# Batch 0's queries in three blocks of 256, one of them mixed of even and odd chunks, in a kernel of clustered attention and a gated feed-forward network

## The chip, the cores and the metric

The kernel runs on one core of a Trainium2 chip. The metric is the device time of one execution in microseconds (us). A core has five engines with a queue each: TensorE (PE, matrix products; the loading of a product's stationary operand is shown apart as PEld), VectorE (DVE), ScalarE (ACT, exponentials and other functions), GpSimd (POOL) and SyncE (SP). Any of SP, ACT and POOL can issue transfers (DMAs), which then run beside the engines. Matrix products write to PSUM, which here has eight banks of 128 rows by 512 numbers of 32 bits.

## What is computed

Four batches (B) of 768 tokens (S) with 8 heads (H) of 64 numbers (D). Each query and key belongs to the nearest of 16 centroids of its head (by the cosine), and a query sees only the keys of its own cluster. The result, 3072 tokens of 512 numbers, goes through a feed-forward network with a sigmoid gate (512 to 1536 and back to 512).

```python
q_assign = argmax(einsum('bhsd,hcd->bhsc', q_n, c_n))      # q_n, k_n, c_n: divided by their norms
k_assign = argmax(einsum('bhsd,hcd->bhsc', k_n, c_n))
mask = q_assign[:, :, :, None] == k_assign[:, :, None, :]
scores = where(mask, q @ k.T / sqrt(D), -1e9)
x = softmax(scores) @ v                                    # to (B * S, H * D)
gate = 1 / (1 + exp(-(x @ w_gate)))
out = (gate * (x @ w_val)) @ w_out
```

## The kernel before, in words

**Attention.** The 768 tokens of a batch are six chunks of 128, three called even and three odd by their number; tile `even` holds keys and queries of the even chunks, `odd` those of the odd ones, transposed, with 64 rows of numbers and 16 rows that mark the cluster (mask rows), so that one product of 80 rows gives the masked score. Heads go in four pairs p = 0 to 3. A block is one batch, one pair and a run of query chunks; it has 12 units, one for each of the two heads and six key chunks. `attend` (L983) takes some units at a time: the score products (L1008) go to a tile `sc` of two PSUM banks, of which there are two; one exponential on ACT (L1032) turns them into `es`; the value products (L1059, 65 columns, the last being the sum) add up in `av`; DVE takes the reciprocal (L1084) and normalises (L1089). The result `xn` is turned into `x`, the input of the network, by a transposing DMA of SP (L1117), or for some blocks by PE (L1097) with a copy of DVE (L1113).

A block of 384 queries takes two units to an exponential (768 columns); one of 256 takes four (1024), one of 128 six (768). The very first block, 256 queries of batch 0 and pair 0, is set to three (`together = 3`). In batches 1 to 3 the blocks are the even and the odd 384 queries. Batch 0 is split to let the network start early: a block of 256 even queries (group (0, 0) of the network), and then, for group (0, 1), the third even chunk by itself (128) and the odd 384.

**Preparing.** Keys and queries are loaded (L334 on SP's queue, some on POOL's), turned by PE (L617, L795 for batch 0's pairs) or by DVE (L595) and scaled (L577 on DVE, L802 on ACT), cast on POOL (L823, L650), multiplied with the centroids (L687, L835), and the one-hot rows of the best centroid are turned (L549, L574) and placed as mask rows, partly by small DMAs of SP (`odd<-even`, `even<-oht`). Weights come in nine loads on POOL's queue, three each of wg, wv and wo, with due times in `WT` (L1647).

**Network.** `feed` (L1409) does a group: for each of 12 chunks of the 1536 the gate products and the value products (L1422, banks called `ring`, of which there are three), tanh on ACT (L1585) and the gating on DVE (L1596). In batches 1 to 3 some of these chunks go in fours by a scheme of seven products in place of eight (L1498, with sums of weights made once at L1403, copies on ACT at L1517 and sums on DVE at L1529 and L1544). The sums of weights stand on DVE's queue around 34 to 50 us. The output projection (`project`, L1187) is done in the same manner for pairs of token chunks (L1275); its argument `many` lets it use the score banks beside the ring, which holds for the last group and for group (B - 1, 0) before it.

**What sets the order.** Nothing of the order is written out. Each of the steps is a task with an engine, a duration, its predecessors, a latency and a due time (`od.add`, `due_at` L319, `due_ffn` L324); the class `Order` (L39) plans all of them in several passes by these numbers and emits each engine's instructions in the planned order. Each engine then runs its queue in that order. So a changed number at one place can move instructions on all engines.

## Time and profile before

| | |
|---|---|
| runs: median (lowest, highest), 3 runs | 315.62 us (315.27, 318.08) |
| the profiled execution's own time | 316.29 us |
| its span, first to last instruction | 314.5 us |
| granted clock of TensorE, mean | 0.999 |
| bytes read, written | 28.34 MB, 6.29 MB |

The lines of the profile that the argument rests on stand in the prediction. A line of the chain of waits or of the time line begins with the start and the length in us; "L1008" is a line of the kernel before; `sc<-even` says which tile is written from which; `x3` counts instructions; in square brackets stands how long the engine was idle before it, and what ended that. Products overlap on TensorE: what one of a row costs is the spacing of their starts, less than the mean duration of one.

### The profile page before, as it was taken

To read this page: it belongs to the slowest core of one execution; us is meant where nothing else is said; L and a number is where in the kernel's file an instruction comes from. 1 tells how busy PE (TensorE), PEld (TensorE's weight loads), DVE (VectorE), ACT (ScalarE), POOL (GpSimd) and SP (SyncE) were. 2 spreads that over 40 slices of the span, in tenths; PEclk is the share of its full clock that TensorE was granted. 3 is DMA by queue.
4 is the path that set the end of the run, shared out by engine and by line. 5 is a ranking of instruction groups with operands and counts; after the bars stand their busy time and mean duration, and the time that the engine had idled before them with its cause. 6 is when DMAs were issued, how large, how long until landed. Compare 5 with 4: busy or idle time off the path is not lost.

```text
span 314.5 us, 8301 instructions
## 1 busy us (share of the span) xinstructions
PE 303.7 (97%) x3251; PEld 223.0 (71%) x3251; DVE 236.5 (75%) x575; ACT 235.0 (75%) x365; POOL 77.5 (25%) x110
## 2 busy tenths in 40 slices
PE   7998899999999999999999999999999999999895
PEld 3677688644578867757776877757777888768674
DVE  4999847799978749885486978977475944786893
ACT  4799899332999979868897768957899778943521
POOL 5897563881011401340002200470000000000000
PEclk9999999999999999999999999999999999999999
DMA  6999999994465886891465683996200022000003
GB/s 216 376 273 150 238 215 121 124 147 68 82 101 105 142 137 176 105 113 40 106 102 88 104 185 94 100 122 59 83 6 15 15 81 79 16 2 36 34 0 133
DMA packets 97430, 34.49 MB, mean 110 GB/s; under 512 B 83136, under 2 KB 93296, under 8 KB 97392
## 3 DMA queue, kind: packets, MB, share of 16 engines
q1 hardware_dynamic: 72048, 24.30, 34.1%
q0 software_dynamic: 24336, 8.65, 27.1%
q10 hardware_dynamic: 1008, 1.02, 0.9%
q8 instruction: 25, 0.41, 0.5%
q14 instruction: 13, 0.11, 0.1%
HBM read 28.34 MB, written 6.29 MB: 110 GB/s over the span
## 4 chain that ended last, share of the span: by engine, by line
PE 83%; ACT 5%; DMA 5%; DVE 5%; issue 1%; DVEq 0%; SPq 0%; ACTq 0%
PE ring L1422 28%; PE sc L1008 17%; PE ring L1275 15%; PE av L1059 9%; PE ring L1498 8%; ACT es L1032 3%; PE sc L687 3%; DMA nat<-in_q_dram 3%; PE sc L1275 2%; DMA out_dram<-out 1%; PE sc L1498 1%; DMA cn<-in_centroids_dram 1%; DVE t L577 1%; DVE even L574 1%; ACT nat L1517 1%
## 5 line engine op out<-in xcount | busy, mean ns | idle before, releaser
L1032 ACT ACTIVATE es<-sc,nbias 128x768 f16<-128x768 f32 (+1 forms) x189 | 168.6, 923 | 18.4 <-PE sc L1008 17.0
L1059 PEld LDWEIGHTS <-es 128*128 128x128 f16 x1152 | 54.9, 97 | 15.0 <-issue 0.2
L1059 PE MATMUL av<-vp,es 128*128 128x65 f16 x1152 | 60.1, 193 | 0.0
L1585 ACT ACTIVATE gt<-ring 128x384 f32<-128x384 f32 (+2 forms) x68 | 34.2, 503 | 33.9 <-PE ring L1422 26.2
L1422 PE MATMUL ring<-x,wv 128*128 128x384 f16 (+2 forms) x272 | 55.3, 325 | 0.1
L1422 PE MATMUL ring<-x,wg 128*128 128x384 f16 (+2 forms) x272 | 55.4, 326 | 0.0
L1596 DVE SCALAR_TENSOR_TENSOR hT<-gt,ring 128x384 f16<-128x384 f32 (+2 forms) x68 | 37.2, 548 | 21.7 <-PE ring L1422 18.1
L650 POOL CAST even<-t 128x768 f16<-128x768 f32 x24 | 20.5, 871 | 118.8 <-DVE t L595 59.7
L1422 PEld LDWEIGHTS <-wv 128*128 128x128 f16 x272 | 25.0, 97 | 15.8 <-issue 0.8
L1422 PEld LDWEIGHTS <-wg 128*128 128x128 f16 x272 | 24.6, 98 | 15.9 <-issue 2.5
L1275 PEld LDWEIGHTS <-hT 128*128 128x128 f16 x294 | 27.1, 98 | 4.6
L1008 PE MATMUL sc<-even 80*128 80x384 f16 (+2 forms) x120 | 26.3, 293 | 1.7 <-ACT es L1032 1.2
L1008 PE MATMUL sc<-odd,even 80*128 80x384 f16 x96 | 26.3, 326 | 0.4 <-ACT es L1032 0.4
L1008 PE MATMUL sc<-odd 80*128 80x384 f16 x96 | 26.4, 325 | 0.1
L1008 PE MATMUL sc<-even,odd 80*128 80x384 f16 (+2 forms) x120 | 26.4, 293 | 0.1
L1008 PEld LDWEIGHTS <-even 80*128 80x128 f16 x216 | 19.9, 98 | 7.5 <-issue 1.6
L1008 PEld LDWEIGHTS <-odd 80*128 80x128 f16 x216 | 19.5, 98 | 7.6 <-issue 2.9
L1529 DVE TENSOR_TENSOR nat<-ring,nat 128x384 f32<-128x384 f32 x26 | 13.9, 551 | 10.1 <-ACT nat L1517 8.6
L1498 PEld LDWEIGHTS <-wss 128*128 128x128 f16 x224 | 19.0, 97 | 3.5 <-issue 1.9
L595 DVE STREAM_TRANSPOSE t<-nat 128x384 f32<-128x384 f32 x40 | 21.4, 556 | 0.0
L334 POOL DMA_DIRECT2D vp<-in_v_dram x24 | 19.7, 833 | 0.1
L1089 DVE TENSOR_TENSOR xn<-av,rr 128x384 f16<-128x384 f32 (+2 forms) x36 | 18.2, 506 | 0.8
(140 smaller groups left out, 456.3 us busy)
## 6 DMA issues: line engine op xcount, KB each, us to landing
out_dram<-out SPq DMA_DIRECT2D x21, 256.0 KB, 2.4
nat<-in_k_dram SPq DMA_DIRECT2D x32, 96.0 KB, 3.0
nat<-in_q_dram SPq DMA_DIRECT2D x32, 96.0 KB, 3.0
odd<-even SPq DMA_DIRECT2D x12, 192.0 KB, 3.2
vp<-in_v_dram POOLq DMA_DIRECT2D x24, 96.0 KB, 4.8
nat<-in_k_dram SPq DMA_DIRECT2D x5, 384.0 KB, 6.9
nat<-in_q_dram SPq DMA_DIRECT2D x5, 384.0 KB, 7.2
nat<-in_v_dram SPq DMA_DIRECT2D x4, 384.0 KB, 6.9
```

What stands on the lines that cost most here:

```text
L334: eng, (0.74 if eng == "POOL" else 0.69) if pkt == 13 else ISSUE[eng], lambda: Q[eng].dma_start(out=out_of(), in_=in_of()),
L595: nc.vector.transpose(t[:, half * QB : (half + 1) * QB].rearrange("p (c x) -> p c x", x=128), blocks_[:, half],)
L650: nc.gpsimd.tensor_copy(t[:, NM[nm], cols], t32[p, nm].tile[:, cols])
L1008: nc.tensor.matmul(out=to, lhsT=kb.tile[0:80, 0, e * QB + j // 2 * 128 : e * QB + (j // 2 + 1) * 128], rhs=qb_.tile[0:80, 1, e * QB + c0 * ...
L1032: i = nc.scalar.activation(to, of, AF.Exp, bias=nbias, scale=D ** -0.5 if quarters(b, p) else scale,).ins
L1059: nc.tensor.matmul(out=av.tile[:, g : g + D + 1], lhsT=es.tile[:, i * N + c * 128 : i * N + (c + 1) * 128], rhs=vp[:, e, j, :], start=firs ...
L1089: nc.vector.tensor_tensor(take(xn)[:, :nq].rearrange("p c (e d) -> p (c e) d", d=D), sums()[:, :, 0:D], rr.tile[:, : 2 * nq].unsqueeze(2). ...
L1275: nc.tensor.matmul(out=ps[:, lo:hi], lhsT=left_()[:, i], rhs=right(i)[:, n0 : n0 + w], start=new and i == 0, stop=i == NFC // 2 - 1, skip_ ...
L1422: nc.tensor.matmul(out=ps[:, :N], lhsT=ws[fc // FPG][:, dcc, fc % FPG, :], rhs=xb.tile[:, dcc, :N], start=(dcc == 0), stop=(dcc == NDC - 1),)
L1498: nc.tensor.matmul(out=ps[:, f], lhsT=w_[:, d, f], rhs=x_()[:, d], start=new and not (f or d), stop=d == 1, skip_group_check=True,)
L1585: lambda rg=rg, gt=gt: nc.scalar.activation(take(gt)[:, :N], rg.tile[:, :N], AF.Tanh, scale=0.5),
L1596: nc.vector.scalar_tensor_tensor(t[:, fc, :N], gt.tile[:, :N], 1.0, rv.tile[:, :N], ALU.add, ALU.mult)
```

## The change

Four things change together.

- The blocks of batch 0. A block is now a tuple of runs of chunks. Group (0, 1) has two blocks of 256 queries: one of the third even chunk and the first odd one, for which each unit has two score products of 128 columns, and one of the other two odd chunks. All of batch 0's blocks are 256 wide and take four units to an exponential, the first one too (`and 0`). The order of the blocks begins with the three of pair 0, then the even 256 of pairs 1, 2 and 3, then the other two of each.
- Banks of the projection. `many` no longer holds for group (B - 1, 0): its products go to the ring's banks alone. (The lines that set `seven` for the last group give what they gave before.)
- Loads. Due times in `WT`: the second wg 23 to 19, a wo 29 to 32, another 43 to 47. The planner's due time for casts of v, and the latency that it counts for loads of batches 1 to 3, 2.0 to 3.0.
- Numbers of the planner: due times and latencies of scores, values, mask rows, sums and products, as in the diff. The whole order is planned anew with them.

By kinds of instructions, TensorE has 48 products more than before (48 scores of 384 columns go, 48 of 256 and 48 of 128 come), ACT 9 exponentials fewer (36 of 768 go, 27 of 1024 come), and 42 projection products write to the ring instead of the score banks. The numbers of DVE's operations and of transposing DMAs are the same. On SP's queue batch 1's second query load stands, as before, behind the transposing DMAs of pair 0's three blocks, but ahead of a small mask copy (`odd<-even`) of pair 2 that was ahead of it; on POOL's the second wg load stands ahead of pair 3's casts, and the first cast of batch 1's keys ahead of the third wg and wv loads.

```diff
--- before
+++ after
@@ -300,15 +300,16 @@
-    SPLIT = ((0, 0, 2), (0, 2, 1), (1, 0, 3))
+    SPLIT = (((0, 0, 2),), ((0, 2, 1), (1, 0, 1)), ((1, 1, 2),))
     groups = {(0, 0): SPLIT[:1], (0, 1): SPLIT[1:]}
...
         for par in range(2):
-            groups[b, par] = ((par, 0, QCH),)
-    blocks = [
-        (0, 0, 0, SPLIT[0]), (0, 1, 0, SPLIT[2]), (0, 1, 0, SPLIT[1]), (0, 0, 1, SPLIT[0]),
-        (0, 0, 2, SPLIT[0]), (0, 0, 3, SPLIT[0]),
-    ]
+            groups[b, par] = (((par, 0, QCH),),)
+
+    def chunks(part):
+        return sum(n for _, _, n in part)
+    blocks = [(0, 0, 0, SPLIT[0]), (0, 1, 0, SPLIT[1]), (0, 1, 0, SPLIT[3 - 1])]
+    blocks += [(0, 0, p, SPLIT[0]) for p in range(1, NP)]
     blocks += [(0, 1, p, part) for p in range(1, NP) for part in SPLIT[1:]]
@@ -317,10 +318,10 @@
     def due_at(slot):
-        return T1 + (slot - S1) * (0.403 if slot < S1 else 0.826)
+        return T1 + (slot - S1) * (0.403 if slot < S1 else 0.825)
     def due_ffn(work):
-        return 38.0 + work * 1.78
+        return 39.0 + work * 1.78
@@ -494,7 +495,7 @@
                 1.05, held, due, acq=[] if held else [buf], uses=[buf] if held else [], early=early,
-                seq=behind, lat=2.0 if b else (0.2 if p == 1 else 1.0),
+                seq=behind, lat=3.0 if b else (0.2 if p == 1 else 1.0),
             )
@@ -741,7 +742,7 @@
                                 [a5, shifted[b, p, half]], due - (20.0 if (b, grp[0]) == (1, 0) else 0),
-                                uses=[oht, aug[b, p][e]], lat=3.2,
+                                uses=[oht, aug[b, p][e]], lat=1.2,
                             )
@@ -762,7 +763,7 @@
                 ),
-                [last, *alloc], lat=0.02, due=due + 0.3 * n_ + (2.0 if n_ > 5 else 0.0), uses=[ohf, aug[b, p][e]],
+                [last, *alloc], lat=0.02, due=due + 0.3 * n_ + (4.0 if n_ > 5 else 0.0), uses=[ohf, aug[b, p][e]],
             )
@@ -984,14 +985,15 @@
         due = due_at(slot)
-        b, gr, p, (par, c0, nq) = block
+        b, gr, p, part_ = block
+        nq = chunks(part_)
         N = 128 * nq
         together = 1024 // N if nq != QCH and 512 % N == 0 and 12 % (1024 // N) == 0 else 768 // N
-        if block == blocks[0]:
+        if block == blocks[0] and 0:
             together = 3
...
         some = UNITS[at : at + together]
-        qb_ = aug[b, p][par]
+        qbs = [aug[b, p][par] for par, _, _ in part_]
         sc, es = Buf("sc"), Buf("es")
@@ -1005,19 +1007,22 @@
                 )
-                nc.tensor.matmul(
-                    out=to,
-                    lhsT=kb.tile[0:80, 0, e * QB + j // 2 * 128 : e * QB + (j // 2 + 1) * 128],
-                    rhs=qb_.tile[0:80, 1, e * QB + c0 * 128 : e * QB + c0 * 128 + N],
-                    start=True, stop=True,
-                )
+                at_ = 0
+                for par, c0, n in part_:
+                    nc.tensor.matmul(
+                        out=to[:, at_ : at_ + 128 * n],
+                        lhsT=kb.tile[0:80, 0, e * QB + j // 2 * 128 : e * QB + (j // 2 + 1) * 128],
+                        rhs=aug[b, p][par].tile[0:80, 1, e * QB + c0 * 128 : e * QB + (c0 + n) * 128],
+                        start=True, stop=True,
+                    )
+                    at_ += 128 * n
...
                     "PE", 0.005 + 0.053333 * nq, score,
-                    masked[b, p, j % 2, "k", e] + masked[b, p, par, "q", e],
+                    masked[b, p, j % 2, "k", e] + [m for par, _, _ in part_ for m in masked[b, p, par, "q", e]],
                     due - (33.5 if early else 0.0), lat=0.25,
-                    acq=[] if i else [sc], uses=[kb, qb_] + ([sc] if i else []),
+                    acq=[] if i else [sc], uses=[kb, *qbs] + ([sc] if i else []),
                     seq=scored_last[-1:],
@@ -1066,7 +1071,7 @@
             value, [t2] + [vload[b, p][e] for e in dict.fromkeys(e for e, _ in some)],
-            due + (-4.1 if last else 5.5) - (19.5 if early else 0.0), lat=0.25 if last else 0.0,
+            due + (-4.1 if last else 5.5) - (21.5 if early else 0.0), lat=0.25 if last else 0.0,
             seq=exps[-1:], acq=[av] if first else [], uses=[es] + ([] if first else [av]),
@@ -1106,7 +1111,7 @@
                 break
-            x0 += 128 * part[2]
+            x0 += 128 * chunks(part)
@@ -1246,7 +1251,7 @@
                         (done1 if done1 is not done2 else []) + done2[: 2 * i1] + list(behind)[n : n + 1],
-                        due - -13.0 - (6.0 if end and not n else 0.0), lat=0.13, acq=fresh, both=True,
+                        due - -15.0 - (6.0 if end and not n else 0.0), lat=0.13, acq=fresh, both=True,
                         uses=hs + [buf for buf in to if buf not in fresh],
@@ -1408,7 +1413,7 @@
         xb, hb = x_of[b, gr], Buf("hT")
-        nt = sum(part[2] for part in groups[b, gr])
+        nt = sum(chunks(part) for part in groups[b, gr])
         N, w = 128 * nt, nt / 3
@@ -1432,6 +1437,8 @@
         seven = WP[: {(0, 0): 0, (0, 1): 0, (1, 0): 2, (1, 1): 2, (2, 0): 2, (2, 1): 3, (3, 0): 3, (3, 1): 2}[b, gr]]
+        if (b, gr) == (B - 1, 1):
+            seven = (2, 4)
         if not wsums_of:
@@ -1502,7 +1509,7 @@
                     "PE", 0.01 + 4 * half / 2400, go, xdone[b, gr] + t_tasks + wsums_of[fa] + deps,
-                    due_ffn(work + step * 0.8), lat=0.25, acq=[r_] if new and not (y and X is Y) else [],
+                    due_ffn(work + step * 0.3), lat=0.25, acq=[r_] if new and not (y and X is Y) else [],
                     uses=[xb, tb] + ([r_] if not new or y and X is Y else []), seq=free + ([m1] if y and new else []),
@@ -1519,7 +1526,7 @@
                 return od.add(
-                    eng, 0.375 if eng == "ACT" else 0.47, go, [m], due_ffn(work) - 5.0, lat=0.16,
+                    eng, 0.375 if eng == "ACT" else 0.47, go, [m], due_ffn(work) - 4.0, lat=0.16,
                     acq=[to] if new else [], uses=[r_] + ([] if new else [to]),
@@ -1548,7 +1555,7 @@
                     od.add(
-                        "DVE", 0.06 + 0.405 * w, go, deps, due_ffn(work) - 10.0, lat=0.14, seq=done[:1],
+                        "DVE", 0.06 + 0.405 * w, go, deps, due_ffn(work) - 14.0, lat=0.14, seq=done[:1],
                         uses=[hb, pu, *uses], both=i == 1,
@@ -1599,13 +1606,13 @@
                 od.add(
-                    "DVE", 0.06 + 0.405 * w, gated, [g2, v1], due - 10.0, lat=0.14, seq=done[:1],
+                    "DVE", 0.06 + 0.405 * w, gated, [g2, v1], due - 14.0, lat=0.14, seq=done[:1],
                     acq=[] if fc else [hb], uses=[gt, rv] + ([hb] if fc else []),
...
         blocks_of = left.pop(b, [])
-        for par, c0, n in groups[b, gr]:
+        for par, c0, n in [run for part in groups[b, gr] for run in part]:
             for c in range(c0, c0 + n):
@@ -1619,7 +1626,7 @@
         pairs = [
-            project(b, blocks_of[i], blocks_of[i + 1], end and i + 2 == len(blocks_of), (end and i > 0) or (b, gr) == (B - 1, 0), end)
+            project(b, blocks_of[i], blocks_of[i + 1], end and i + 2 == len(blocks_of), end and i > 0, end)
             for i in range(0, len(blocks_of), 2)
@@ -1642,9 +1649,9 @@
         load_nat(0, p_, "q", "SP", -7.9 + p_, behind=nat[0, p_, "k"])
-        load_v(0, p_ - 1, "SP", -7.8 + p_, 20.0 + 4.5 * p_, behind=nat[0, p_, "q"])
-    load_v(0, NP - 1, "SP", -7.7 + p_, 20.0 + 4.5 * NP, behind=nat[0, NP - 2, "v"])
-    WT = (12.5, 16.0, 23.0, 24.0, 29.5, 29.5, 38.0, 29.0, 43.0)
+        load_v(0, p_ - 1, "SP", -7.8 + p_, 19.5 + 4.5 * p_, behind=nat[0, p_, "q"])
+    load_v(0, NP - 1, "SP", -7.7 + p_, 19.5 + 4.5 * NP, behind=nat[0, NP - 2, "v"])
+    WT = (12.5, 16.0, 19.0, 24.0, 29.5, 29.5, 38.0, 32.0, 47.0)
     n = 0
@@ -1655,7 +1662,7 @@
     for p_ in range(1, NP):
-        prepare_pair(0, p_, (0, 10.0, 13.5, 18.5)[p_], 0.24, (('k', 'q'), (), ('k', 'q'))[p_ - 1], p_ in (1, 2, 3))
+        prepare_pair(0, p_, (0, 10.0, 14.0, 18.5)[p_], 0.24, (('k', 'q'), (), ('k', 'q'))[p_ - 1], p_ in (1, 2, 3))
     od.behind(first_turn[1], [q0])
@@ -1673,12 +1680,12 @@
                         )
-                prepare(b + 1, grp, max(due - 27.5, 45.5) + (9.0 if (b, grp[0]) == (0, 2) else 0), 1.31)
+                prepare(b + 1, grp, max(due - 32.5, 45.5) + (9.0 if (b, grp[0]) == (0, 2) else 0), 1.31)
         at = 0
...
             at += n
-            slot += n * part[2] / QCH
+            slot += n * chunks(part) / QCH
         done[b, gr] = done.get((b, gr), 0) + 1
...
             if b + 1 < B:
```

Lines of the changed kernel are numbered some 1 to 7 higher than the same ones before.

## Prediction

> **What bounds the kernel now.** The page comes first: busy shares, granted clock, chain.
>
> ```profile
> span 314.5 us, 8301 instructions
> PE 303.7 (97%) x3251; PEld 223.0 (71%) x3251; DVE 236.5 (75%) x575; ACT 235.0 (75%) x365; POOL 77.5 (25%) x110
> PE 83%; ACT 5%; DMA 5%; DVE 5%; issue 1%; DVEq 0%; SPq 0%; ACTq 0%
> ```
>
> TensorE (PE) is busy for 97% of the span and carries 83% of the chain. A change can gain only where PE works less or stands still. Where it stands still, the view by stretches says:
>
> ```profile
> core 0: us, PE busy (x) PEld busy (x) DVE busy (x) ACT busy (x) POOL busy (x), PEclk, DMA share, GB/s
> 20.00:25.00 5.00, 4.94 (x67) 3.60 (x65) 4.69 (x13) 5.00 (x8) 4.88 (x8) 1.00 1.19 247
> 25.00:30.00 5.00, 4.15 (x69) 3.62 (x70) 4.67 (x14) 4.65 (x5) 4.67 (x7) 1.00 1.12 126
> 30.00:35.00 5.00, 3.93 (x61) 3.26 (x57) 4.65 (x13) 4.98 (x6) 1.65 (x2) 1.00 1.19 233
> 35.00:40.00 5.00, 4.18 (x59) 3.35 (x60) 3.94 (x12) 3.77 (x6) 3.58 (x5) 1.00 1.23 225
> 60.00:278.00 218.00, 217.82 (x2328) 158.30 (x2327) 164.65 (x372) 174.77 (x270) 35.88 (x44) 1.00 0.58 91
> 280.00:290.00 10.00, 9.70 (x83) 7.64 (x82) 7.86 (x19) 3.03 (x7) 0.00 (x0) 1.00 0.01 2
> 290.00:300.00 10.00, 9.20 (x75) 6.54 (x74) 7.74 (x19) 5.23 (x13) 0.00 (x0) 1.00 0.15 54
> ```
>
> In each row the first number behind the comma is PE's busy time in the stretch; the clock is 1.00 in all. From 60 to 278 us PE lacks 218.00 − 217.82 = 0.18 us: nothing is to be had there. From 20 to 40 it lacks 0.06 + 0.85 + 1.07 + 0.82 = 2.80 us, from 280 to 300 it lacks 0.30 + 0.80 = 1.10. In the first of these DVE is packed as well (4.65 to 4.69 of 5.00 from 20 to 35), and ACT nearly so. What PE waits for, in 20 to 40 (first two rows) and 278 to 300 (the others):
>
> ```profile
> PE sc L1008 <- ACT es L1032: 1.6, 4, 0.7
> PE ring L617 <- DMA nat<-in_q_dram: 1.2, 1, 1.2
> ...
> PE sc L1498 <- DVE nat L1529: 0.5, 1, 0.5
> PE sc L1498 <- ACT p L1517: 0.3, 1, 0.3
> PE ring L1097 <- DVE hT L1544: 0.2, 1, 0.2
> PE sc L1498 <- ACT nat L1517: 0.2, 1, 0.2
> ```
>
> The first group is 2.8 us in five stops, the second 1.2 in four. The longest stop is followed back by the chain and by SP's queue:
>
> ```profile
> 26.79 8.49 DMA nat<-in_q_dram
> ...
> 35.41 0.52 PE ring L617 x3
> ...
> 38.15 0.49 PE sc L1008 x2
> ```
> ```profile
> 25.54 1.15 SPq L1117 DMA_TRANSPOSE x<-xn  x1
> 26.79 1.44 SPq L334 DMA_DIRECT2D nat<-in_q_dram  x1
> ```
>
> The queries of batch 1, heads 2 and 3, are issued at 26.79, behind the transposing DMA of x of batch 0's 128-query block, and land 8.49 us later. PE turns them at 35.41, its scores fall behind, and a score product waits for an exp again at 38.15. So the phase up to batch 0's first FFN product is bound by order and arrival, not by PE's work.
>
> **The change, part by part.** *Blocks of batch 0.* The blocks of 384 and 128 queries become two of 256, one of them an even and an odd chunk of 128, that is two 128-wide products for each unit. With 48 units (12 for each of four pairs of heads), 48 products of 384 and none of 128 go, 48 of 256 and 48 of 128 come, each for odd and even keys together: 48 more products in all. Prices by spacing:
>
> ```profile
> 40.13 0.34 PE sc L1008 x6
> ...
> 271.27 0.33 PE sc L1008 x2
> ...
> 303.05 1.31 PE ring L1275 x12
> ```
>
> Six 128-wide scores take 0.34 us (0.057 each), two 384-wide ones 0.33 (0.165), twelve 256-wide products 1.31 (0.109). So 48 × (0.057 + 0.109 − 0.165) = +0.05 us; I carry +0.1. All are on the path, since PE is the bound. Bounds: 0, and 48 × (0.219 + 0.272 − 0.325) = 8.0 us by the mean durations of one product of 128, 256 and 384, a price that overlapping products don't pay. The Trainium skill speaks against this split (TensorE: Matmul & The Clock Gate, Back-to-back issue gap): a sustained stream of weight loads and products is said to take about 81 ns for each at 128 columns. By that rule the 48 extra 128-wide products would cost 48 × (81 − 57) ns, an estimate of +1.2 us. The row of six above, where every product has its own weight load, shows 57 ns, so the trace sides against the rule here.
>
> ACT gets fewer and wider exps: 36 of 768 go, 27 of 1024 come.
>
> ```profile
> L1032 ACT ACTIVATE es<-sc,nbias 128x768 f16<-128x768 f32 x180 | 159.3, 913 | 18.0 <-PE sc L1008 16.6 <-PE av L1059 0.2
> L1032 ACT ACTIVATE es<-sc,nbias 128x1024 f16<-128x1024 f32 x9 | 9.5, 1119 | 0.3 <-PE sc L1008 0.3
> ```
>
> 36 × 0.913 − 27 × 1.119 = 2.7 us of ACT at the most, and about half by spacing. It counts 0 by itself: ACT waits 16.6 us for scores and is not the bound; it enters below as one of the things that may close the 1.6 us stops. No exp count changes in batches 1 to 3.
>
> *Earlier query load, order of the first 40 us.* In the changed order SP has the transposing DMAs of the two new 256-query blocks, then the load, then pair 2's small mask copy, which the next blocks need only some 10 us later. It stays behind a transposing DMA whose input DVE makes, so I put the issue at 25.5 to 26.0 instead of 26.79; with 8.49 us it lands at 34.0 to 34.5. PE comes to the turn after the same work as before, so about 34.2. Of the 1.2 us stop up to 0.3 stays. But DVE is packed, and decides what comes next:
>
> ```profile
> 27.83 0.37 DVE L574 STREAM_TRANSPOSE even<-ohf 32x192 f32<-32x192 f32 x1
> ...
> 31.75 1.48 DVE L577 TENSOR_SCALAR t<-ring 128x384 f32<-128x384 f32 x3
> ...
> 37.43 0.42 DVE L1113 CAST x<-ring 128x256 f16<-128x256 f32 x1
> ```
>
> Before, pair 3's query mask rows (27.83) end just ahead of its scores. The new order moves two copies of batch 1's keys (L577, about 0.47 apart by the row of three) and some smaller work ahead of these rows: about 1.5 us more. Pair 3's scores then start about 1.4 us later, but PE has about 1.4 us more work in front of them, so this stop (the 0.7 us of the exp row) stays as it is. Behind it lies the copy of x that the first FFN product waits for. Adding DVE's operations in the new order, each at the median of its kind, puts it at 32.3 us of work. In the old order it began at 37.43 after 32.1 us of work, 5.3 behind, and other copies between 14 and 37 us stood 4.1 to 5.3 behind; at 4.7 it begins at 37.0 and ends at 37.4. PE then starts the FFN at 37.5 after 29.7 us of work (7.8 behind), where before it started at 39.5 after 30.6 (8.9 behind). Gain 1.1, of which I take −1.0: 0.9 from the query stop, 0.1 from the exp stop behind it. Bounds: 0 if that load lands as late as now, −2.8 if all five stops go.
>
> *Weight loads.* The second gate weight goes ahead of pair 3's four casts on POOL, the second value weight behind them, and wo later.
>
> ```profile
> 22.09 1.59 POOL L823 CAST even<-t 64x768 f16<-64x768 f32 x2
> 23.74 1.60 POOL L823 CAST odd<-t 64x768 f16<-64x768 f32 x2
> 25.28 0.74 POOL L334 DMA_DIRECT2D wg<-in_moe_w_gate_dram  x1
> 26.01 0.75 POOL L334 DMA_DIRECT2D wv<-in_moe_w_val_dram  x1
> ```
>
> One 0.74 us issue is thus put in front of the casts and pair 3's key rows get 0.7 us later on POOL; they are ready at 25.3, then 26.0, while DVE's rows of that pair end near 29, so the cover is 3 us. The value load's issue stays near 26.5. Counted 0; what it costs when it lands late is the third rival.
>
> *Middle.*
>
> ```profile
> 70.64 2.97 SPq L334 DMA_DIRECT2D even<-oht  x4
> 73.66 2.48 SPq L334 DMA_DIRECT2D odd<-oht  x4
> ```
>
> Batch 1's centroid products come 2.5 us earlier in PE's order; its first scores too. From 60 to 278 us PE lacks 0.18 us now, so no gain is possible, and a loss only where a mask row comes late. Now the last of them are issued on SP from 70.64 to 73.66 + 2.48 = 76.14, and they move with the products. I count 0, bounds 0 and +0.6 (two stops as long as the 0.3 of the tail's rows). The products L1275 of group (3,0) go to the FFN's banks instead of the scores': 42 products, the same count and width, 0 on PE.
>
> *Tail.* With those products off the score banks, the next group's first Strassen-like products (L1498) needn't wait for the draining of the projection. That takes away the 0.3 stop, and the new order parts the products of the 0.2 one. The 0.5 us stop stays: a product that needs the sum L1529 of one before it.
>
> ```profile
> 290.70 0.49 ACT nat L1517
> ...
> 291.22 0.57 DVE nat L1529
> ```
>
> A copy and a sum, 1.08 us with hand-overs, lie between two products on one bank, and the new order puts only two other products there. −0.6 with the restart after each stop (0.1 each); bounds 0 and −1.2, all four.
>
> **Sum.** Against the profiled execution's own time, 316.29 us (span 314.5): −1.0 + 0.1 + 0 − 0.6 = 314.8. That execution lies 0.67 above the median of the three runs (315.62), so the forecast is 314.1 us, 0.5% less.
>
> **The rivals.** *A, the query load is hidden no better.* SP's two transposing DMAs may wait for DVE as long as now, or the load may take over 9 us beside the earlier weight load (DMA share 1.12 to 1.23 in 20 to 40). Then the first term is 0: 316.29 + 0.1 − 0.6 − 0.67 = 315.1 us. For it: DVE's 4.65 of 5.00. Against it: the load has one queue entry less ahead of it.
>
> *B, all goes.* With 1024-wide exps from the start, ACT runs ahead and its stops (1.6) vanish with the load's (1.2), and the tail's 1.2: 316.29 − 2.8 + 0.1 − 1.2 − 0.67 = 311.7 us. Against it: pair 3's scores wait for DVE's rows, which aren't earlier.
>
> *C, the other side: the second value weight lands late.*
>
> ```profile
> L334 POOL DMA_DIRECT2D wv<-in_moe_w_val_dram x3: 740/747/762, 16.1 to 29.0; - x3
> ...
> DMA to landing us min/median/max: 9.4/10.7/16.9
> ```
>
> In the new order DVE sums this weight (L1403) ahead of its first gating product (L1596), in order. That gating product is needed about 2 us after its turn, when the FFN's three banks are full: near 41 us. Issued at 26.5 and landing 10.7 later, the weight costs nothing; from 14 on it decides, and at the longest landing seen, 16.9, the sum ends at 26.5 + 16.9 + 0.4 = 43.8, and PE stops 2.8 us. 314.1 + 2.8 = 316.9 us, slower than before by 0.4%. Before, the same sums stood behind 37.97 us and the gating products waited for none.
>
> **How the numbers follow.** Forecast 0.47, A 0.20, B 0.14, C 0.14, and 0.05 for something unseen in the middle. The likeliest case's own range is 313.0 to 315.2 (the first term from −0.4 to −1.5, the tail from −0.2 to −1.2). The range to state, 312.0 to 317.0, takes A and C in whole and leaves out the far end of B and a wait in the middle that adds to C. About 1% (3.2 us) is what a measurement of this kernel can tell from no change; faster than 312.5 needs B nearly whole: 0.12. Slower than 318.8 needs C and more: 0.06. Within: 0.82.
>
> **What would show it.** Right: the query load issued before 26.2 and PE's stop before its turn (L617) under 0.4 us; the first FFN product near 37.5; score pairs of 128 still 0.057 apart; from 60 to 278 PE lacks under 0.5 us; in 280 to 300 it lacks about 0.6. Wrong: the load lands after 35; DVE's first gating product waits for the weight sum; a mask row or a centroid product stops PE past 60 us; the 128-wide pairs take 0.08 each.

## The result, and the profile after

The changed kernel takes 314.38 us (median of 20 runs, 313.36 to 319.3) against 316.36 for the kernel before (20 runs); the ratio is 0.9938, with a 95% interval of 0.9923 to 0.9953. It is 0.6% faster, within the 1% that the prediction called about the size of what can be told apart, and 0.3 us from the time on record. Medians here are of all runs; the ratios leave out a few slow ones (the 319.3 us is one), in which the granted clock was lower. The profiled execution of the changed kernel took 313.98 us, with a span of 312.1.

The page of the changed kernel, busy shares and chain:

```profile
span 312.1 us, 8367 instructions
PE 304.1 (97%) x3299; PEld 226.0 (72%) x3299; DVE 235.8 (76%) x575; ACT 233.1 (75%) x356; POOL 77.2 (25%) x110
PE 88%; DVE 5%; ACT 2%; DMA 1%; issue 1%; SPq 0%; DVEq 0%
```

PE's busy time is the same, 304.1 against 303.7. On the chain its share rose from 83% to 88% and that of DMA fell from 5% to 1%. The stretches (columns as before the change):

```profile
20.00:25.00 5.00, 4.76 (x66) 4.21 (x65) 4.75 (x12) 4.89 (x8) 4.84 (x8) 1.00 1.18 250
25.00:30.00 5.00, 4.41 (x69) 3.35 (x66) 4.81 (x13) 3.67 (x4) 4.90 (x7) 1.00 1.71 131
30.00:35.00 5.00, 4.39 (x65) 3.64 (x64) 4.44 (x13) 4.47 (x5) 2.01 (x3) 1.00 1.11 194
35.00:40.00 5.00, 5.00 (x84) 4.59 (x82) 4.51 (x14) 5.00 (x7) 3.59 (x5) 1.00 1.23 226
60.00:278.00 218.00, 217.33 (x2327) 157.62 (x2325) 163.77 (x372) 173.97 (x269) 35.40 (x44) 1.00 0.58 91
280.00:290.00 10.00, 9.50 (x94) 8.36 (x92) 7.46 (x17) 4.70 (x11) 0.00 (x0) 1.00 0.11 41
290.00:300.00 10.00, 9.99 (x73) 6.57 (x71) 9.01 (x23) 4.37 (x9) 0.00 (x0) 1.00 0.04 15
```

From 20 to 40 us PE lacks 0.24 + 0.59 + 0.61 + 0 = 1.44 us where it lacked 2.80; from 280 to 300 it lacks 0.51 where it lacked 1.10; in the middle 0.67 where it lacked 0.18. What PE waits for in 20 to 40 (three rows), 60 to 278 (one) and 276 to 300 (one):

```profile
PE av L1064 <- DVE xn L1094: 0.8, 2, 0.6
PE sc L1012 <- ACT es L1037: 0.3, 1, 0.3
PE sc L1012 <- DVE even L575: 0.3, 1, 0.3
...
PE sc L1012 <- DMA even<-oht: 0.4, 1, 0.4
...
PE sc L1505 <- DVE nat L1536: 0.5, 1, 0.5
```

The stop for the query load is gone, three of the tail's four are gone, and a mask row now comes 0.4 us late in the middle. The load and the first FFN product, from the time lines of SP and PE, with the load's time to landing between them:

```profile
25.52 0.53 SPq L335 DMA_DIRECT2D nat<-in_q_dram  x1
...
DMA to landing us min/median/max: 8.5/8.5/8.5
...
37.39 0.60 PE L1427 MATMUL ring<-x,wg 128*128 128x256 f16 x4
```

The load lands at 25.52 + 8.5 = 34.0; PE starts the FFN at 37.39, where it was 39.53.

### The profile page after: what moved, and what is told of

The parts are those of the page before. It is cut to its first block, busy times and chain, and to the rows that moved or that the text cites. A ratio compares the mean times of both kernels' runs of the same rounds, so it can differ in the third digit from the quotient of the medians.

```text
span 312.1 us, 8367 instructions
## 1 busy us (share of the span) xinstructions
PE 304.1 (97%) x3299; PEld 226.0 (72%) x3299; DVE 235.8 (76%) x575; ACT 233.1 (75%) x356; POOL 77.2 (25%) x110
## 4 chain that ended last, share of the span: by engine, by line
PE 88%; DVE 5%; ACT 2%; DMA 1%; issue 1%; SPq 0%; DVEq 0%
PE ring L1427 28%; PE sc L1012 19%; PE ring L1280 16%; PE av L1064 10%; PE ring L1505 8%; PE sc L688 2%; DMA even<-oht 1%; PE sc L1280 1%; ACT es L1037 1%; DVE even L575 1%; PE sc L1505 1%; DVE t L578 1%; PE av L360 1%; PE ring L904 1%; DVE nat L1536 1%
## 5 line engine op out<-in xcount | busy, mean ns | idle before, releaser
L1064 PEld LDWEIGHTS <-es 128*128 128x128 f16 x1152 | 53.3, 97 | 13.6 <-issue 1.4
L1064 PE MATMUL av<-vp,es 128*128 128x65 f16 x1152 | 58.3, 193 | 0.8 <-DVE xn L1094 0.8
L1012 PE MATMUL sc<-even 80*128 80x384 f16 (+2 forms) x120 | 28.0, 294 | 1.7 <-DVE even L575 0.8
L1012 PE MATMUL sc<-odd 80*128 80x384 f16 (+2 forms) x120 | 28.6, 293 | 0.1
L1012 PEld LDWEIGHTS <-even 80*128 80x128 f16 x240 | 20.9, 98 | 10.5 <-issue 4.1
L1012 PE MATMUL sc<-odd,even 80*128 80x384 f16 (+2 forms) x120 | 28.3, 294 | 0.0
L1012 PE MATMUL sc<-even,odd 80*128 80x384 f16 (+2 forms) x120 | 27.2, 293 | 0.0
L1012 PEld LDWEIGHTS <-odd 80*128 80x128 f16 x240 | 21.2, 98 | 7.7 <-issue 2.0
L1280 PEld LDWEIGHTS <-s 128*128 128x128 f16 x198 | 18.5, 98 | 3.2 <-DVE s L1249 0.2
```

What stands on the lines that cost most here:

```text
L1012: nc.tensor.matmul(out=to[:, at_ : at_ + 128 * n], lhsT=kb.tile[0:80, 0, e * QB + j // 2 * 128 : e * QB + (j // 2 + 1) * 128], rhs=aug[b, ...
L1064: nc.tensor.matmul(out=av.tile[:, g : g + D + 1], lhsT=es.tile[:, i * N + c * 128 : i * N + (c + 1) * 128], rhs=vp[:, e, j, :], start=firs ...
L1280: nc.tensor.matmul(out=ps[:, lo:hi], lhsT=left_()[:, i], rhs=right(i)[:, n0 : n0 + w], start=new and i == 0, stop=i == NFC // 2 - 1, skip_ ...
```

## The experiments

Twelve kernels were run. All starts in this table are from the time lines of the profiled execution: the first score product, the first FFN product, the last score product, the last product of all. "Tail" is the last column of starts less the one before it. The ratio is to the kernel before as it ran in the same series (its medians there are 316.21 to 316.45 us), with its interval; it is not the quotient of two medians of the table.

| kernel | first score | first FFN | last score | last product | tail | median us (runs) | ratio |
|---|---|---|---|---|---|---|---|
| before | 10.76 | 39.53 | 274.62 | 310.71 | 36.09 | 316.36 (20) | |
| changed | 10.63 | 37.39 | 272.33 | 308.33 | 36.00 | 314.38 (20) | 0.9938 (0.9923 to 0.9953) |
| b_load_first | 10.51 | 38.04 | 273.13 | 309.22 | 36.09 | 315.09 (12) | 0.9957 (0.9941 to 0.9973) |
| b_banks | 10.58 | 39.51 | 274.61 | 309.86 | 35.24 | 315.05 (8) | 0.995 (0.9932 to 0.9969) |
| b_load_banks | 10.68 | 38.13 | 273.17 | 308.41 | 35.24 | 314.06 (5) | 0.994 (0.9928 to 0.9953) |
| b_new_blocks | 10.39 | 37.92 | 274.31 | 310.41 | 36.09 | 315.17 (12) | 0.9964 (0.9948 to 0.998) |
| a_banks_back | 12.08 | 39.21 | 273.65 | 309.87 | 36.23 | 314.32 (6) | 0.9931 (0.9905 to 0.9957) |
| a_old_blocks | 10.57 | 38.03 | 272.09 | 308.09 | 36.01 | 314.0 (6) | 0.9919 (0.9898 to 0.994) |
| a_old_blocks_load_first | 10.49 | 38.37 | 272.37 | 308.37 | 36.00 | 314.16 (6) | 0.9948 (0.9928 to 0.9969) |
| a_load_first | 10.45 | 37.20 | 272.98 | 308.98 | 36.00 | 315.61 (12) | 0.9976 (0.9953 to 1.0) |
| a_old_weights | 10.43 | 37.71 | 272.27 | 308.28 | 36.01 | 313.8 (10) | 0.9933 (0.9912 to 0.9955) |
| a_three_128 | 10.65 | 37.42 | 273.18 | 309.07 | 35.89 | 315.4 (10) | 0.9981 (0.9965 to 0.9996) |
| a_wv_late | 12.05 | 39.18 | 281.38 | 317.39 | 36.00 | 323.34 (2) | 1.023 (1.0196 to 1.0263) |
| a_wv_late_sums_later | 10.93 | 38.09 | 273.58 | 309.58 | 36.00 | 315.04 (8) | 0.9988 (0.9953 to 1.0024) |

Names with b start from the kernel before, names with a from the changed one. A first score at 12 instead of 10.5 us is a start in which a load of the first keys landed 0.6 us later (at 4.8 instead of 4.2 us); two profiled executions had that, so differences of starts are compared and not the starts. Two of these stretches hold different work in different kernels. With the old blocks some 0.75 us more of products, by spacing, lie ahead of the first FFN product than with the new ones; and all kernels with the new numbers have 12 more products of 192 columns (0.082 us apart, 1.0 us) behind the last score. So the first FFN product is compared among kernels with the same blocks, and the tail among those with the same numbers.

**The load alone, in the old order (b_load_first).** One SP instruction, batch 1's second query load (`nat[1, 1, "q"]`), is moved one place; every other queue keeps its order.

```diff
         order = self.schedule()
+        i = order.index(self.first)
+        j = max(n for n in range(i) if order[n].eng == "SP")
+        order.insert(j, order.pop(i))
         for t in order:
...
+    od.first = nat[1, 1, "q"][0]
```

> The kernel before, every queue in its order, but batch 1's second query load is issued one place earlier on SP, ahead of the transposing DMA of the 128-query block. Theory (the query stop is on the path): the load is issued near 25.5 instead of 26.8, PE's stop of 1.15 us before its turn falls to 0 to 0.3, the first FFN product starts near 38.6 to 38.9 instead of 39.5, and the time falls by 0.6 to 0.9 us (ratio to before 0.997 to 0.998). Rival (DVE's order governs that phase, the stop only moves to the next one): the stop before the turn goes, but the first FFN product starts after 39.2, and the time falls by less than 0.3 us.

Its issue and landing, then PE's waits from 20 to 40 us:

```profile
25.18 0.52 SPq L337 DMA_DIRECT2D nat<-in_q_dram  x1
...
DMA to landing us min/median/max: 4.6/4.6/4.6
```
```profile
PE sc L1011 <- ACT es L1035: 1.5, 4, 0.7
```

The row of the load is gone from the waits, the stops for exps stay at 1.5 (1.6 before). From the first score to the first FFN product it takes 27.53 us instead of 28.77, so 1.24 less, and nothing is given back: the rest of the program is the same to 0.02 us. The time fell by more than the expected 0.6 to 0.9 us, to 315.09 against 316.45 in this series. The rival, that DVE would only move the stop on, falls. The load came 5.5 us earlier for an issue 1.6 us earlier, because its 8.49 us became 4.6. The transfers of SP's queue (q1) from 26 to 28 us, in the kernel before and then in this one:

```profile
q0 software_dynamic: 67, 0.07, 58.6%
q1 hardware_dynamic: 135, 0.04, 31.4%
```
```profile
q1 hardware_dynamic: 377, 0.38, 88.0%
...
q0 software_dynamic: 9, 0.01, 2.0%
```

The columns are packets, MB and share of the 16 engines. Here SP's queue moved 0.38 MB, about the size of the load, in these two microseconds, with POOL's queue (q0) almost empty; before, it moved 0.04 MB.

**The banks alone (b_banks, a_banks_back).** The edit in the kernel before, and its reverse in the changed kernel:

```diff
-            project(b, ..., (end and i > 0) or (b, gr) == (B - 1, 0), end)
+            project(b, ..., end and i > 0, end)
```

> The kernel before with the change of banks alone: the projection of group (3, 0) goes to the ring's banks only. Everything up to some 270 us stays as it was. Theory (the score banks are held by that projection): PE's named waits from 276 to 300 us fall from 1.2 us to 0.5 to 0.7, and the time falls by 0.5 to 1.1 us (ratio 0.9965 to 0.9985). Rival (the tail's gain comes from the new due times of products and sums, the banks by themselves do nothing, since ring banks are then scarcer): waits stay at 1.0 us or more and the time changes by less than 0.3 us.

> The changed kernel with that projection back on the score banks as well; the order up to some 275 us is that of the changed kernel. Theory (banks): 0.5 to 1.1 us slower than the changed kernel, so a ratio to before of 0.9955 to 0.9975. Rival (due times): as the changed kernel, 0.9938.

PE's waits from 276 to 300 us, first in b_banks, then in a_banks_back:

```profile
PE sc L1498 <- DVE nat L1529: 0.5, 1, 0.5
PE ring L1097 <- DVE hT L1544: 0.2, 1, 0.2
```
```profile
PE sc L1505 <- DVE nat L1536: 0.4, 1, 0.4
PE sc L1505 <- ACT p L1524: 0.3, 1, 0.3
```

In the kernel before, the edit takes away the stop behind ACT's p that the prediction named and one of the two small ones; the tail is 0.85 us shorter, as the theory had it; the median fell by 1.4, more than the expected 0.5 to 1.1. Undone in the changed kernel, the same stop of 0.3 comes back and the tail is 0.23 longer, but the time is no longer (314.32 against 314.38). So there the theory's 0.5 to 1.1 was too much and the rival (due times) holds: in the new order little else hangs on the banks. Which of the new due times does that was not tried.

**Both edits together (b_load_banks).**

> The kernel before with the two single edits together: the query load one place earlier on SP, and the projection of group (3, 0) on the ring's banks alone. By themselves they shortened the stretch up to the first FFN product by 1.24 us and the tail by 0.85 us. Theory (two separate stops, and together they make nearly all of the change's gain): they add, the first score to the last product takes 297.9 us instead of 299.95, ratio 0.992 to 0.9945. Rival (the time saved early is lost before the end, or the tail's gain needs the old phase): ratio 0.995 or more.

PE's waits in 20 to 40 us (first row) and 276 to 300:

```profile
PE sc L1011 <- ACT es L1035: 1.5, 4, 0.7
...
PE sc L1501 <- DVE nat L1532: 0.5, 1, 0.5
PE ring L1100 <- DVE hT L1547: 0.3, 1, 0.3
```

They add: from the first score to the last product 308.41 − 10.68 = 297.73 us instead of 299.95, 2.2 less (1.24 + 0.85 = 2.09). The ratio is 0.994, that of the whole change. An order of one place on SP and one bank rule, in the old blocks with the old numbers, give as much as everything together (297.69 us in the changed kernel). The medians add less well: 1.36 and 1.40 us alone, 2.15 together, so half a microsecond between two medians says little here.

**The blocks alone, and everything but the blocks (b_new_blocks, a_old_blocks).**

```diff
-    SPLIT = (((0, 0, 2),), ((0, 2, 1), (1, 0, 1)), ((1, 1, 2),))
+    SPLIT = (((0, 0, 2),), ((0, 2, 1),), ((1, 0, 3),))
...
-    blocks = [(0, 0, 0, SPLIT[0]), (0, 1, 0, SPLIT[1]), (0, 1, 0, SPLIT[3 - 1])]
+    blocks = [(0, 0, 0, SPLIT[0]), (0, 1, 0, SPLIT[2]), (0, 1, 0, SPLIT[1])]
...
-        if block == blocks[0] and 0:
+        if block == blocks[0]:
```

This is a_old_blocks; b_new_blocks has the new lines and all numbers, loads and banks of before.

> The changed kernel's numbers, loads and banks, with batch 0 split as before (256, 384, 128; three units to an exponential in the first block). SP's queue then has pair 2's small mask copy and the third transposing DMA ahead of the query load, as before. Theory (the blocks carry the gain of the first 40 us, because they make room for the earlier query load): PE stops before the turn of that load again by 0.7 us or more, and 1.0 to 1.5 us of the 1.4 us gained by 40 us are gone: ratio to before 0.997 to 0.999. Rival (the planner's numbers carry it): first FFN product near 37.6 as in the changed kernel, ratio 0.994 to 0.995.

> The kernel before with the new blocks of batch 0 alone (three of 256, 1024-wide exponentials from the start); all other numbers, loads and banks as before. In its planned order the query load stands ahead of the transposing DMA of the third block. Theory (the blocks matter only by the place that the load gets): no stop before the turn of that load, the stretch from the first score to the first FFN product is 1.0 us or more shorter than in the kernel before, the tail after the last score is its 36.1 us, and the ratio is 0.995 to 0.997. Rival (blocks and widths carry nothing, or cost): ratio 0.998 to 1.001. Second rival (fewer exps by themselves speed the phase up as well): first FFN product before 37.0, ratio under 0.9945.

PE's waits from 20 to 40 us in a_old_blocks:

```profile
PE sc L1012 <- ACT es L1037: 0.9, 2, 0.6
```

The theory that the blocks carry the early gain falls. With the old blocks under the new numbers there is no stop for the load at all, 0.9 us of waits are left instead of the changed kernel's 1.4, and the ratio is 0.9919. There the load is issued at 26.51 and lands 8.1 us later, at 34.6, and PE turns it at 34.85; so it is just in time. The new blocks under the old numbers give 0.9964, as the theory expected from the place of the load (SP issues it at 24.20); its profiled execution, at 315.97 us 0.8 above the median of its runs, shows no load stop and a first FFN product 1.24 us earlier from the first score, of which 0.75 is work moved behind it, but no gain from the first score to the last product (300.02 against 299.95), so how the timed microsecond comes about there isn't shown by its trace. The blocks, and the numbers with the loads' due times, each remove the same stop; together they don't add.

**One place earlier in the changed kernel too (a_load_first, a_old_blocks_load_first).** The edit is that of b_load_first.

> The changed kernel with the query load one place earlier still, ahead of the transposing DMA of the third 256-query block. Theory (the changed kernel no longer stops for this load): the load lands some 4 us earlier (in about 5 us instead of 8.5) and the time stays within 0.3 us of the changed kernel, ratio 0.992 to 0.995. Rival (the load still sets that phase through its copies on DVE): the first FFN product starts before 37.0 us and the time falls by 0.4 us or more.

> The changed kernel's numbers, loads and banks with the old blocks of batch 0, and the load one place earlier on SP. With the old blocks there was no stop for the load either. Theory: as the old blocks alone under the new numbers, 313.7 to 314.3 us, ratio 0.991 to 0.9945, so not slower than the changed kernel: the new blocks contribute nothing to it. Rival: the new blocks are worth something that the first run with old blocks hid; ratio over 0.995.

Neither is faster than without the edit. Of a_load_first neither the theory's ratio nor the rival's first FFN product (before 37.0) came. The load is issued at 23.88 and still lands 9.6 us later, at 33.5:

```profile
DMA to landing us min/median/max: 9.6/9.6/9.6
```

So the expected 5 us was wrong: an early place on SP is no quick landing by itself. Issued before 24, it moved 0.30 MB on SP's queue only from 30 to 32 us, with POOL's queue (the second gate weight had been issued at 20.5) at 98% and more from 24 to 28. Which of the transfers holds it there was not tried apart. From the first score to the first FFN product it took 26.75 us against 26.76, and its median is above the changed kernel's (ratios 0.9976 and 0.9938); its profiled execution shows the late mask row with 0.9 us. With the old blocks the load, issued at 25.64 ahead of the transposing DMA, also took 8.6 us. There 314.16 us came out, inside the theory's range, with a ratio of 0.9948 between the theory's 0.9945 and the rival's 0.995: the changed kernel's new blocks are worth nothing that these runs can tell.

**The loads' due times (a_old_weights).** `WT` as before, all else changed.

> The changed kernel with the weights' old due times; the wo load then stands ahead of the third gate and value weights on POOL, as before. Theory (the late value weight of rival C): DVE needs about 2.2 us from that weight's landing to the next normalisation, which PE waits for at about 46.2 us; the weight lands 2 to 4 us later than the 43.5 of the changed kernel, so PE stops 1.5 to 3.5 us near 46 to 49, and the time is 1.5 to 4 us over the changed kernel, 316 to 318. Rival (the place of the loads is hidden, as the prediction's sum had it): within 0.4 us of the changed kernel, ratio 0.993 to 0.995.

The rival holds: 313.8 us, 0.9933. The order, planned anew, also moved DVE's sums of the third value weight to 46.6 us, so that nothing waited for it. The query load stops PE by 1.0 us again in this kernel (PE's waits from 20 to 40 us):

```profile
PE ring L618 <- DMA nat<-in_q_dram: 1.0, 1, 1.0
```

Still its first FFN product starts at 37.71: some of that stop is covered by others that shrank, and from the first score to the last product it takes 297.85 us against 297.69. So in the new order that stop can come back without the whole getting longer.

**The price of a 128-wide product (a_three_128).**

```diff
-                for par, c0, n in part_:
+                for par, c0, n in [(par, c0 + i_, 1) for par, c0, n in part_ for i_ in range(n)] if b else part_:
```

> The changed kernel, but each score product of 384 columns in batches 1 to 3 is issued as three of 128 with the same weights loaded three times: 576 more products, the order and everything else the same. Theory (a 128-wide product costs its 0.0565 us of spacing): 288 x (3 x 0.0565 - 0.1645) = +1.4 us over the changed kernel, so about 315.8 us. Rival (the Trainium skill's sustained 81 ns at 128 columns, TensorE: Matmul & The Clock Gate, Back-to-back issue gap): 288 x (0.243 - 0.1645) = +23 us, about 337 us.

From its chain of waits:

```profile
200.54 0.17 PE sc L1012 x3
...
205.23 0.34 PE sc L1012 x6
```

Three 128-wide products in 0.17 us, six in 0.34: 0.057 each, with a weight load for each. The time is 1.0 us above the changed kernel (315.4 against 314.38), where spacing gives +1.4 (the changed kernel's profile has a 0.4 us stop for a mask row that this one's has not) and the Trainium skill's 81 ns (TensorE: Matmul & The Clock Gate, Back-to-back issue gap) an estimate of +23. That figure does not hold for this stream, and the prediction's +0.1 for 48 more products stands.

**A late value weight (a_wv_late, a_wv_late_sums_later).**

```diff
         order = self.schedule()
+        order.remove(self.late)
+        order.insert(order.index(self.past) + 1, self.late)
...
+    od.late, od.past = wload["v"][2], wload["o"][0]
```

The third value weight's load is put behind a wo load. The second kernel also moves DVE's four sums of that weight behind its work up to 60 us.

> The changed kernel, but POOL issues the third value weight's load after the wo load that stood at 37.3, some 8 us later; all queues' other orders as they were, so DVE's four sums of that weight still stand ahead of its third gating product. Theory (rival C of the prediction as a mechanism): the weight lands near 49 to 52 instead of 43.5, DVE waits for it, the three banks fill and PE stops 4 to 8 us before 53; time 318 to 322 us. Rival (PE has other work, banks enough): PE stops under 1 us and the time stays within 1 us of the changed kernel.

> As the one before (late third value weight), but DVE's four sums of that weight are moved behind its other work up to 60 us. Theory (the in-order sums are what stops PE): no gating product waits for the weight, PE stops only if the value products of the last third of the FFN come before the weight, by 0 to 1 us; time within 1 us of the changed kernel. Rival (the weight itself is what PE waits for): stop and time as in the one before.

In a_wv_late, DVE's queue and then PE's, and PE's clock by stretches:

```profile
50.48 0.42 DVE L1410 TENSOR_TENSOR wss<-wv 128x512 f16<-128x512 f16 x1 [6.73 <-DMA wv<-in_moe_w_val_dram]
```
```profile
52.75 1.04 PE L1066 MATMUL av<-vp,es 128*128 128x65 f16 x16 [4.78 <-DVE xn L1096]
```
```profile
48.00:50.00 2.00, 0.00 (x0) 0.00 (x0) 0.00 (x0) 1.60 (x2) 0.00 (x0) 1.00 2.62 109
51.00:52.00 1.00, 0.00 (x0) 0.00 (x0) 1.00 (x5) 0.00 (x0) 1.00 (x2) 0.54 2.06 200
54.00:57.00 3.00, 3.00 (x28) 2.61 (x26) 0.70 (x3) 1.50 (x2) 3.00 (x5) 0.50 1.05 180
56.00:58.00 2.00, 2.00 (x15) 1.68 (x14) 1.65 (x5) 0.97 (x2) 2.00 (x4) 0.52 0.85 133
58.00:60.00 2.00, 2.00 (x34) 1.83 (x32) 0.36 (x2) 2.00 (x3) 0.30 (x1) 1.00 1.37 116
```

DVE waits 6.73 us for the weight in order, behind it stands the normalisation xn (L1096), and PE's next value product waits for the bank that xn frees: 4.78 us. From the first FFN product to the last score it takes 242.20 us instead of 234.93, 7.3 more, since PE then runs at half the clock until some 57.9 us: about 5.2 us that do the work of 2.6, and 4.78 + 2.6 = 7.4. The stop lies within the expected 4 to 8 us; the time, 323.34 us, lies above the expected 318 to 322, which had no slower clock in it. With the sums moved away the same late weight costs 235.49 − 234.93 = 0.6, which is one wait of a product for a gating, and the median is 315.04. So the mechanism of rival C is shown, with another weight and at another bank than the prediction said.

## Why the prediction was right, point by point

*The query stop.* Right in kind and size. The load was issued at 25.52 (forecast 25.5 to 26.0), landed at 34.0 (34.0 to 34.5), and PE did not stop for it. That this stop was on the path is shown by b_load_first: 1.24 us by it alone. Rival A falls. That 8.49 us would be the load's time wherever it stands was luck: in other places it was 4.4 to 9.7. Nor does the stop alone decide the time of the new order: in a_old_weights it came back with 1.0 us, and the time did not rise.

*The first 40 us.* The first FFN product was forecast at 37.5 and started at 37.39; DVE's copy ahead of it was forecast to begin at 37.0 and began at 36.77. The product started 2.14 us earlier than in the kernel before, with some 0.75 us less of products ahead of it by spacing, where the prediction counted 0.9: the term −1.0 was −1.4. Two parts were too small. Of the query stop (1.15) "up to 0.3 stays", and none did; and the exp stop behind it, at 38.15 (0.41), was counted with 0.1 and went altogether. "This stop (the 0.7 us of the exp row) stays as it is" held in size and not in kind: PE now waits 0.6 us for DVE's normalisation at 29.0, where it waited 0.65 for an exp at 28.4, and a new stop for mask rows (0.3) comes at 31.0.

*The blocks.* Their price, +0.1, was right and is nearly nothing. The prediction gave them no gain of their own either; a_old_blocks and b_load_banks bear that out.

*The loads' due times.* Counted 0, and a_old_weights shows 0. But the cover was thin, see below.

*The middle.* Counted 0 with a bound of +0.6; measured, a mask row stops PE for 0.4 us near 131 us. That is one of the prediction's signs of being wrong, and PE lacks 0.67 us from 60 to 278 where under 0.5 was to show it right. The planner was told 1.2 us of latency for such rows instead of 3.2, and here they took 2.2 to 5.1 to land. The stop isn't in every run: in a_banks_back, in the same order there, the first of these rows took 4.4 us instead of 5.1, and PE doesn't stop; in a_load_first it took 5.6, and the stop is 0.9. In the sum the middle still gives nothing: from the first FFN product to the last score it takes 234.93 us instead of 235.09, for 0.1 us less of products.

*The tail.* Forecast −0.6, with the 0.5 us stop staying. That stop stayed, and the others went as said. Behind the last score lie 34.7 us of products by spacing, 33.7 in the kernel before; so the tails, 36.00 and 36.09 us, hold 1.3 us in which PE falls behind that work, where it was 2.4: −1.1. The step "−0.6 with the restart after each stop" was sized too low. And the banks are not the only cause: they alone leave 35.24 − 33.7 = 1.5 us in the old order, but so does the new order with the score banks given back (a_banks_back, 36.23 − 34.7 = 1.5). Either gives most of it, and in the changed kernel the banks add 0.2.

*The sum and the median.* Two errors cancelled, so that the time came out within 0.3 us is luck in part. The forecast's steps made −1.5 us. The measured ones make −1.4 + 0.1 + 0 − 1.1 = −2.4, where the two profiled executions differ by 2.3 and the medians of 20 runs each by 2.0. And the profiled execution, put 0.67 above the median by three runs, stands at the median of 20 (316.29 against 316.36). With the right offset the same steps would have given 314.9.

*Rival B.* It falls: 1.4 us of stops are left from 20 to 40 us, and 0.5 in the tail.

*Rival C.* It was given the second value weight and the FFN's banks. The second was in time (DVE sums it at 38.67). The third was the late one: issued at 28.87, waited for by DVE from 41.96 to 43.54, as the row shows.

```profile
43.54 0.42 DVE L1408 TENSOR_TENSOR wss<-wv 128x512 f16<-128x512 f16 x1 [1.58 <-DMA wv<-in_moe_w_val_dram]
...
45.34 0.41 DVE L1094 TENSOR_TENSOR xn<-av,rr 128x256 f16<-128x256 f32 x1
```

xn is done at 45.75, and PE needs it at about 46.0 (in a_load_first, where the weight lands 0.5 us later, xn ends at 46.24 and the value product starts at 46.30). So the changed kernel has about 0.2 us to spare there. Whether any of its timed runs used that up is not shown.

## What to carry to other kernels

When a large rearrangement gains little, look for the one or two waits that it happened to remove, and remove them alone: here one place in a queue and one bank rule, in the old order, gave as much as the whole. That shows what is enough, not what the new order needs: there one place more gave nothing, and the bank rule 0.2 us. A transfer's time to landing belongs to its place among the other transfers; forecast it with a span, not with the number of the old place. And work of no hurry that waits in order for a transfer should not stand ahead of work that the bound engine needs: its slack is the slack of the whole program.

## What was not expected of the hardware

A stop of PE cost more than its length where it was long. In a_wv_late the granted clock stays 1.00 for 3.1 us of the 4.78 us stop (until 51.1 us), falls to 0.54 in the stretch from 51 to 52 us and 0.50 after it, and is back at 1.00 only at 57.9 us, 5.2 us after PE's restart; 128-wide products are then 0.107 us apart instead of 0.056. The short stops of all other kernels here, up to 1.2 us, show no such thing. The Trainium skill (TensorE: Matmul & The Clock Gate, What's actually happening) gives at least one window of about 3.4 us of idling before the clock is halved, and at least one of sustained work before it is whole; the trace shows a little less for the first (3.1 us) and 5.2 for the second.
